# A fused attention and two-MLP kernel: early stage by batch, operand tile 384 bytes further on

## The chip, the cores and the metric

One core of one Trainium2 chip runs the whole program. The metric is device time in microseconds of one execution; a profiled execution gives the trace, in which the span runs from the first to the last instruction. Engines: PE (TensorE, matmuls), DVE (VectorE), ACT (ScalarE), POOL (GpSimd), and SP, whose queue starts the transfers.

## The reference

Three layers follow each other. B = 4 batches, 8 heads, S = 576 rows, head size 64, 32 memory slots; then NT = 2304 tokens of width 512.

```python
a = softmax(phi, axis=2)                        # b h s m, over m
k_m = einsum('bhsm,bhsd->bhmd', a, k); v_m = einsum('bhsm,bhsd->bhmd', a, v)
attn = softmax(q @ k_m.T / 8, axis=-1)          # over the 32 slots
x = (attn @ v_m)                                # -> 2304 x 512 tokens
x = relu(x @ w_in)**2 @ w_out                   # d_ff = 2048, weights are float64
p = probs / sum(probs)
out = sum_e p[:, e] * (relu(x @ w1[e]) @ w2[e]) # 4 experts, d_ff = 1024 each
```

## The kernel before, in words

Products of full precision are made of fp32r matmuls: an operand x is kept as a high part and a remainder (`put`, `split`), and a product is three matmuls (high·high, high·rest, rest·high).

**Early stage (slab 0).** The eight groups g are (batch, half of the heads). `front(g)` (F in the program string) loads phi, K/V and q, makes the memory (lines 121 to 163) and the scores: two halves z of 288 columns, each into a PSUM bank with the tag "score", of which there is one, and from there by a DVE transpose into `st` (line 173). Step B is the rest of the group: maximum, subtract (line 177), exponential, sum, reciprocal, multiply (line 185), transpose to `at` (line 189), the high part (ACT, line 191) and the remainder (DVE, line 192) into `mem`. Step A is `fold(0, b)`, which multiplies the first weights into the values of batch b. Step U j is the first MLP's slab 0 on half a batch (j = 0 and 1 are batch 0, and so on): `first_l1` (line 320) reads the attention tile of both groups of the batch, and the second layer `first_l2` (line 342) of a step is issued behind the first layer of the next one. Step W converts one chunk of 128x512 float64 weights to fp32 (`from_f64`, seven DVE instructions, lines 206 to 218) and, for the second layer, splits it (lines 231, 232). `PROGRAM` is the order in which these steps are written; the layer that builds the program then interleaves them on each engine, and each engine runs its list strictly in order. `FIRST_LOADS` is the order of the first transfers on the one queue of SP (p = phi, q, r = raw float64 weights, k = K/V).

**Slabs 1 to 4** of the first MLP follow, with `fold(s, b)` for each slab (line 296; its results leave PSUM through ACT line 302 and DVE line 303).

**Second stage.** The second MLP runs in two passes of 16 slabs. `second_pair` multiplies seven combinations of input blocks (moving operand, 512 columns, in the slots of `mem`) with seven combinations of weights (stationary, line 470); `second_l2` (line 431) has the second weights as the moving operand (512 columns, tiles `w` of other pools) and the activations `g` as the stationary one; `second_rest` (line 516) takes the last 256 columns, also out of `mem`. GpSimd makes the weight combinations (lines 266 to 269).

`mem`, one tile of 73,728 bytes per partition, holds the attention and the folded weights in the first MLP, and the slots of the second. The pool `const` hands out its tiles one behind the other: `ident` (512 bytes), `mem`, `acc`, and then the two small tiles of the probabilities.

Of the kernel before, what the change touches and what calls it, by code (L numbers as in the profile page):

```python
# [12 lines left out]
F32 = mybir.dt.float32  # L13
F32R = mybir.dt.float32r
AF = mybir.ActivationFunctionType
ALU = mybir.AluOpType
AX = mybir.AxisListType
I32 = mybir.dt.int32
U32 = mybir.dt.uint32

B, H, S, D, M = 4, 8, 576, 64, 32
NT, DM, DFF, E, F2 = 2304, 512, 2048, 4, 1024
KT = DM // 128
NG = 8
WC = 512
# [13 lines left out]
def tile_kernel(  # L39
# [10 lines left out]
    nc = tc.nc  # L50
    const = ctx.enter_context(tc.tile_pool(name="const", bufs=1))
    wcp = ctx.enter_context(tc.tile_pool(name="wcp", bufs=8))
# [7 lines left out]
    def bank(tag):  # L60
        return ps.tile([128, 512], F32, tag=tag, name=tag, bufs=BANKS[tag])

    ident = const.tile([128, 128], F32, name="ident")
    make_identity(nc, ident)

# [3 lines left out]
    atts = [a[:, 0] for a in area]  # L71
# [1 line left out]
    slot = [mem[:, i * 4 * NB:(i + 1) * 4 * NB] for i in range(9)]  # L73
    acc = const.tile([128, NT * KT], F32, name="acc")
    yacc = acc.rearrange("p (k n) -> p k n", k=KT)
    p_sb = const.tile([128, NT // 128, E], F32, name="p_sb")
    p_sum = const.tile([128, NT // 128], F32, name="p_sum")


    FIRST_LOADS = "p0 q0 r0 k0 p1 r1 k1 q1 r2 r3"  # L80

    PROGRAM = (
        "F0 W W F1 B0 A0 B1 F2 U0 W W F3 U1 B2 A1 B3 F4 U2 F5 U3 W B4 A2 B5 F6 U4 W F7 U5 "
        "B6 A3 B7 W U6 W U7"
    )


    CH = [(r * 128, min(128, S - r * 128)) for r in range((S + 127) // 128)]  # L90
# [5 lines left out]

    def load_kv(att, g):
        kvt = []
        for c, (s0, n) in enumerate(CH):
            if g == 0 and c < KT:  # L100
                t = yacc[:, c, S:S + 8 * D].rearrange("p (z h d) -> p z h d", z=2, h=4)
            else:
                t = att.tile([128, 2, 4, D], F32, tag="kv", name=f"kv{g}_{c}", bufs=5)
            nc.sync.dma_start(out=t[:n], in_=kv[g, s0:s0 + n].rearrange("s (z h d) -> s z h d", z=2, h=4))
            kvt.append(t)
        return kvt
# [10 lines left out]
    def attention(att, g):  # L117
        b, hg = divmod(g, 2)
        ph, kvt, qt = phs[g], kvs[g], qs[g]
        nmax = att.tile([128, 1], F32, tag="nmax", name="nmax")  # L120
        nc.vector.tensor_reduce(out=nmax, in_=ph, axis=AX.X, op=ALU.max, negate=True)
        esum = att.tile([128, 1], F32, tag="esum", name="esum")
        nc.scalar.activation(ph, ph, AF.Exp, bias=nmax, scale=1.0, accum_out=esum)
        rs = att.tile([128, 1], F32, tag="rs", name="rs")
        nc.vector.tensor_scalar_add(rs, esum, 1e-9)
        nc.vector.reciprocal(rs, rs)
        en = att.tile([128, len(CH), 128], F32, tag="en", name="en", bufs=1)
        pa = bank("turn")
        pb = bank("memory")
        for c, (s0, n) in enumerate(CH):  # L130
            dst = pa[:n, c * 128:(c + 1) * 128] if c < 4 else pb[:n, :128]
            nc.tensor.transpose(dst, ph[:, s0:s0 + n], ident)
        nc.scalar.copy(en[:, 0:4].rearrange("p c m -> p (c m)"), pa)
        nlast = CH[-1][1]
        nc.scalar.copy(en[:nlast, 4], pb[:nlast, :128])
        kvp = pb[:, 128:256]
        for c, (s0, n) in enumerate(CH):
            for h in range(4):
                nc.tensor.matmul(  # L139
                    kvp[h * M:(h + 1) * M, :2 * D],  # L140
                    en[:n, c, h * M:(h + 1) * M],
                    kvt[c][:n, :, h, :],
                    start=(c == 0),
                    stop=(c == len(CH) - 1),
                )


        kvd = att.tile([128, 2, 2, D], F32, tag="kvd", name="kvd", bufs=1)
        nc.scalar.activation(
            kvd,  # L150
            kvp.rearrange("p (v d) -> p v d", v=2).unsqueeze(2).to_broadcast([128, 2, 2, D]),
            AF.Copy, scale=rs,
        )
        kt = pb[:, 256:512]
        for v in range(2):
            nc.tensor.transpose(kt[:, v * 128:(v + 1) * 128], kvd[:, v].rearrange("p z d -> p (z d)"), ident)
        bt = bdk[g % 2]
        ktv = kt.rearrange("p (v z e m) -> p v z e m", v=2, z=2, e=2)
        for e in range(2):
            rows = slice(e * D, (e + 1) * D)  # L160
            nc.scalar.copy(bt[rows, :, e * M:(e + 1) * M], ktv[rows, 0, :, e, :])
        rows = slice(hg * D, (hg + 1) * D)
        nc.scalar.copy(vt[rows, b], kt[rows, 128:])
        st = att.tile([128, S // 32, 32], F32, tag="st", name="st", bufs=2)
        stf = st.rearrange("p j m -> p (j m)")
        for z in range(2):
            sc = bank("score")
            for pr in range(2):
                nc.tensor.matmul(
                    sc[pr * 64:(pr + 1) * 64, :HS], bt[:, pr, :], qt[pr][:, z * HS:(z + 1) * HS],  # L170
                    start=True, stop=True,
                )
            nc.vector.transpose(out=stf[:, z * HS:(z + 1) * HS], in_=sc[:, :HS])
        yield
        mx = att.tile([128, S // 32], F32, tag="mx", name="mx")
        nc.vector.reduce_max(out=mx, in_=st, axis=AX.X)
        nc.vector.tensor_tensor(
            out=st, in0=st, in1=mx.unsqueeze(2).to_broadcast([128, S // 32, 32]), op=ALU.subtract
        )
        nc.scalar.activation(st, st, AF.Exp, scale=1.0 / math.sqrt(D))  # L180
        sm = att.tile([128, S // 32], F32, tag="sm", name="sm")
        nc.vector.reduce_sum(out=sm, in_=st, axis=AX.X)
        nc.vector.tensor_scalar_add(sm, sm, 1e-9)
        nc.vector.reciprocal(sm, sm)
        nc.vector.tensor_tensor(
            out=st, in0=st, in1=sm.unsqueeze(2).to_broadcast([128, S // 32, 32]), op=ALU.mult
        )
        at = att.tile([128, S], F32, tag="at", name="at", bufs=1)
        nc.vector.transpose(out=at, in_=stf)
        hi = atts[b][:, hg]  # L190
        nc.scalar.copy(hi, at)  # L191
        nc.vector.tensor_tensor(out=atts[b][:, 2 + hg], in0=at, in1=hi.bitcast(F32), op=ALU.subtract)

# [4 lines left out]
    def from_f64(r, w):  # L200
        lo, hi = r[:, :, 0], r[:, :, 1]
        m = cv.tile([128, WC], F32, tag="cm", name="cm")
        a = cv.tile([128, WC], U32, tag="ca", name="ca")
        if w is None:
            w = a.bitcast(F32)
        nc.vector.tensor_scalar(m.bitcast(U32), hi, 0x7FFFFFFF, None, op0=ALU.bitwise_and)
        nc.vector.tensor_scalar(m, m, F_MIN, F_MAX, op0=ALU.max, op1=ALU.min)
        nc.vector.tensor_scalar(
            a, m.bitcast(U32), 3, 0x3FFFFFFF, op0=ALU.logical_shift_left, op1=ALU.bitwise_and
        )  # L210
        nc.vector.scalar_tensor_tensor(
            out=a, in0=hi, scalar=0xC0000000, in1=a, op0=ALU.bitwise_and, op1=ALU.bitwise_or
        )
        nc.vector.tensor_scalar(m.bitcast(U32), a, 0xFF800000, None, op0=ALU.bitwise_and)
        nc.vector.scalar_tensor_tensor(
            out=m, in0=lo, scalar=2.0 ** -52, in1=m, op0=ALU.mult, op1=ALU.mult
        )
        nc.vector.tensor_tensor(out=w, in0=a.bitcast(F32), in1=m, op=ALU.add)
        return w
# [312 lines left out]
    phs, kvs, qs, raws = {}, {}, {}, {}  # L532
# [7 lines left out]
    with tc.tile_pool(name="bdp", bufs=1) as bdp, tc.tile_pool(name="cv", bufs=1) as cv, \  # L540
# [6 lines left out]
        with tc.tile_pool(name="att", bufs=2) as att, tc.tile_pool(name="hp1", bufs=2) as hp, \  # L547
                tc.tile_pool(name="tmp1", bufs=1) as tmp:
            at = {}

            def front(g):
                if g not in phs:
                    phs[g] = load_phi(att, g)
                if g not in kvs:
                    kvs[g] = load_kv(att, g)
                if g not in qs:
                    qs[g] = load_q(g)
                at[g] = attention(att, g)
                next(at[g])

            for t in FIRST_LOADS.split():
                i = int(t[1])
                if t[0] == "p":
                    phs[i] = load_phi(att, i)
                elif t[0] == "k":
                    kvs[i] = load_kv(att, i)
                elif t[0] == "q":
                    qs[i] = load_q(i)
                else:
                    raws[i] = load64(i)  # L570
            for t in PROGRAM.split():
                i = int(t[1]) if len(t) > 1 else 0
# [17 lines left out]
            out=p_sb, in0=p_sb, in1=p_sum.unsqueeze(2).to_broadcast([128, NT // 128, E]), op=ALU.mult  # L590
# [98 lines left out]
```

## Time and profile before

| | before |
|---|---|
| median of 3 runs | 1167.53 us (1166.3 to 1167.62) |
| profiled execution | 1166.94 us; span 1164.9 us; granted clock 0.994 |
| PE busy / DVE / ACT / POOL | 98% / 72% / 42% / 10% |
| PE busy, 20 to 60 us | 30.94 of 40.00 us |
| PE busy, 440 to 700 us | 260.00 of 260.00 us |

A profile is read from the stretches: PE's busy time is modelled for pipelined matmuls, so that a busy PE need not run at its full rate. The rate is seen from the starts of successive matmuls. Where PE isn't busy, the row of the instruction behind the gap says what ended the wait.

### The profile page before, as it was taken

The page shows a single profiled execution, that of the slowest core. Times are in us where ns is not written, and L with a number is a line of the kernel's source. Part 1 is how long each engine was busy: PE and PEld are TensorE (multiplying, and loading weights), DVE is VectorE, ACT ScalarE, POOL GpSimd, SP SyncE. Part 2 cuts the span into 40 slices and gives each one's busy share as a digit, 9 for nine tenths or more (in the row PEclk, how much of TensorE's full clock was granted, in tenths as well). Part 3 has the DMA queues.
Part 4 walks back from the last instruction along what each step waited for, and adds up shares of the span by engine and source line. Part 5 has one row for each costly group of instructions (what it writes and reads, how often), then busy time and mean ns, then how long its engine had stood idle before and what let it go on. Part 6 is the DMA issues. An engine that isn't in the chain of part 4 may idle for free.

```text
span 1164.9 us, 16690 instructions
## 1 busy us (share of the span) xinstructions
PE 1139.3 (98%) x6520; PEld 957.9 (82%) x6520; DVE 839.0 (72%) x1442; ACT 494.9 (42%) x1051; POOL 121.3 (10%) x136
## 2 busy tenths in 40 slices
PE   5899999999999999999999999999999999999998
PEld 2676898999999988888888888888888888888886
DVE  5988999887457667777777778856666666666654
ACT  2666555544466563343433434543333333332321
POOL 0000000001010022121121211211111111121000
PEclk9799999999999999999999999999999999999999
DMA  9751222211000111111111111311111111111002
GB/s 313 237 184 37 73 74 91 74 55 55 1 19 1 54 46 64 37 55 55 55 55 37 55 55 53 110 37 37 37 37 54 37 55 37 37 37 37 19 1 91
DMA packets 25599, 72.68 MB, mean 62 GB/s; under 512 B 2992, under 2 KB 3504, under 8 KB 25520
## 3 DMA queue, kind: packets, MB, share of 16 engines
q1 hardware_dynamic: 25520, 71.61, 18.5%
q8 instruction: 51, 0.84, 0.3%
q14 instruction: 28, 0.23, 0.1%
HBM read 66.88 MB, written 4.72 MB: 61 GB/s over the span
## 4 chain that ended last, share of the span: by engine, by line
PE 91%; DVE 6%; ACT 1%; issue 1%; DMA 1%; SPq 0%; ACTq 0%
PE moe L470 23%; PE fold L431 17%; PE memory L431 8%; PE moe L342 8%; PE turn L431 8%; PE moe L320 4%; PE moe L516 4%; PE score L470 4%; PE turn L342 2%; PE score L342 2%; PE memory L342 2%; PE fold L296 2%; PE memory L320 1%; PE score L320 1%; PE memory L139 1%; DVE acc L350 1%
## 5 line engine op out<-in xcount | busy, mean ns | idle before, releaser
L431 PE MATMUL fold<-w,g 128*128 128x512 f32 x864 | 221.4, 391 | 0.0
L470 PE MATMUL moe<-mem,ws 128*128 128x512 f32 x768 | 201.4, 397 | 0.8 <-DVE c L478 0.8
L431 PEld LDWEIGHTS fold<-w,g 128*128 128x128 f32 x864 | 160.2, 188 | 33.2
L470 PEld LDWEIGHTS moe<-mem,ws 128*128 128x128 f32 x768 | 142.7, 188 | 37.9 <-DVE c L478 5.4
L342 PE MATMUL moe<-gh,wo 128*128 128x288 f32 x576 | 130.8, 298 | 1.2 <-ACT acc L348 0.7
L442 DVE SCALAR_TENSOR_TENSOR acc<-fold,p_sb,acc 128x512 f32<-128x512 f32 x135 | 100.8, 747 | 40.4 <-PE fold L431 40.2
L266 POOL TENSOR_TENSOR s<-ra 128x256 f32<-128x256 f32 x32 | 27.2, 850 | 951.5 <-DVE ws L232 391.3
L483 ACT COPY cc<-moe 128x512 f32<-128x512 f32 x96 | 56.1, 584 | 149.6 <-PE moe L470 149.4
L431 PE MATMUL turn<-w,g 128*128 128x512 f32 x432 | 110.1, 390 | 0.0
L431 PE MATMUL memory<-w,g 128*128 128x512 f32 x432 | 109.9, 390 | 0.0
L452 DVE SCALAR_TENSOR_TENSOR g<-c,g 128x512 fp32r<-128x512 f32 x128 | 97.4, 779 | 16.2 <-ACT g L451 11.8
L451 ACT ACTIVATE g<-c 128x512 fp32r<-128x512 f32 x128 | 80.3, 633 | 67.5 <-DVE c L478 66.8
L478 DVE TENSOR_TENSOR c<-moe,cc 128x512 f32<-128x512 f32 x96 | 66.0, 688 | 57.1 <-ACT cc L483 37.0
L342 PEld LDWEIGHTS moe<-gh,wo 128*128 128x128 f32 x576 | 97.4, 189 | 6.5 <-ACT acc L348 2.5
L431 PEld LDWEIGHTS turn<-w,g 128*128 128x128 f32 x432 | 81.1, 188 | 17.4
L431 PEld LDWEIGHTS memory<-w,g 128*128 128x128 f32 x432 | 81.1, 188 | 17.4
L470 PE MATMUL moe<-mem,w 128*128 128x512 f32 x384 | 95.3, 395 | 0.0
L470 PEld LDWEIGHTS moe<-mem,w 128*128 128x128 f32 x384 | 71.9, 188 | 17.0 <-ACT cc L483 0.2
L342 PE MATMUL moe<-gl,wo 128*128 128x288 f32 x288 | 85.6, 297 | 0.0
L320 PE MATMUL moe<-mem 128*128 128x288 f32 x432 | 75.3, 307 | 7.4 <-ACT mem L191 7.4
L231 ACT CAST w<-rb 128x512 fp32r<-128x512 f32 x64 | 39.9, 623 | 97.5 <-PE memory L431 65.8
L320 PEld LDWEIGHTS moe<-mem 128*128 128x128 f32 x432 | 62.3, 192 | 20.8 <-issue 9.8
(119 smaller groups left out, 1830.3 us busy)
## 6 DMA issues: line engine op xcount, KB each, us to landing
ra<-in_wts SPq DMA_DIRECT2D x32, 512.0 KB, 3.5
rb<-in_wts SPq DMA_DIRECT2D x32, 512.0 KB, 3.5
raw<-in_wts SPq DMA_DIRECT2D x28, 512.0 KB, 3.4
kv<-in_kv SPq DMA_DIRECT2D x28, 256.0 KB, 4.8
acc<-in_qT SPq DMA_DIRECT2D x16, 288.0 KB, 5.2
out<-acc SPq DMA_DIRECT2D x18, 256.0 KB, 2.0
ph<-in_phiT SPq DMA_DIRECT2D x8, 288.0 KB, 4.6
acc<-in_wts SPq DMA_DIRECT2D x4, 512.0 KB, 6.1
```

The costliest lines, as they stand in the source:

```text
L231: nc.scalar.copy(t[:, 0], w)
L266: nc.gpsimd.tensor_tensor(out=t[:, 0], in0=a21, in1=a22, op=ALU.add)
L320: nc.tensor.matmul(ph[:, :HS], folded[b][:, lw + hg, fc], atts[b][:, rx + hg, cs], start=(i == 0), stop=(i == 5))
L342: nc.tensor.matmul(po[:, :HS], w[:, lw], rg[:, f], start=(i == 0), stop=(i == 3 * nf - 1))
L431: nc.tensor.matmul(po, g[f][:, lg, at:at + 128], w[:, rw], start=(i == 0), stop=(i == 3 * NF2 - 1))
L442: nc.vector.scalar_tensor_tensor(out=oa, in0=src, scalar=pe, in1=oa, op0=ALU.mult, op1=ALU.add)
L451: nc.scalar.activation(g[:, 0, :n], c, AF.Relu)
L452: nc.vector.scalar_tensor_tensor(out=g[:, 1, :n], in0=c, scalar=0.0, in1=g[:, 0, :n].bitcast(F32), op0=ALU.max, op1=ALU.subtract)
L470: nc.tensor.matmul(po, wb[lw][k], xb[:, rx, k], start=(first and i == 0), stop=(i == 5), skip_group_check=not first,)
L478: nc.vector.tensor_tensor(out=c, in0=p, in1=q, op=ALU.add)
L483: nc.scalar.copy(c, p)
L516: nc.tensor.matmul(ph[:, :NR], w[f][:, lw, k * 128:(k + 1) * 128], x[:, rx, k], start=(i == 0), stop=(i == 3 * KT - 1),)
```

## The change

- `PROGRAM` is rewritten: two fronts, then both groups' B, then two steps U, batch by batch; four conversions W stand ahead of A0.
- `FIRST_LOADS`: both phi first, q of group 0 behind its K/V. The K/V of group 1 goes to three free weight buffers in place of the `kv` buffers.
- Scores: the second half of a group goes to a bank with the tag "fold", no longer to the one with the tag "score".
- For groups 4 to 7 the subtract, the multiply and the remainder run on GpSimd; for group 3 the multiply does.
- `from_f64`: the first DVE instruction of a chunk (clear the sign bit) becomes an ACT activation Abs.
- The tiles of the probabilities are taken ahead of `mem`. In the built program `mem` then starts at byte 17,408 of a partition (17 x 1024) in place of 17,024 (16 x 1024 + 640), and `acc` at 91,136 in place of 90,752. The tiles of the other pools keep their places: the weight buffers start at 128,000 (125 x 1024), the second stage's `g` at 201,728 (197 x 1024).

```diff
+    p_sb = const.tile([128, NT // 128, E], F32, name="p_sb")
+    p_sum = const.tile([128, NT // 128], F32, name="p_sum")
...
-    p_sb = const.tile([128, NT // 128, E], F32, name="p_sb")
-    p_sum = const.tile([128, NT // 128], F32, name="p_sum")
...
-    FIRST_LOADS = "p0 q0 r0 k0 p1 r1 k1 q1 r2 r3"
+    FIRST_LOADS = "p0 p1 r0 k0 r1 q0 k1 q1 r2 r3"
...
-        "F0 W W F1 B0 A0 B1 F2 U0 W W F3 U1 B2 A1 B3 F4 U2 F5 U3 W B4 A2 B5 F6 U4 W F7 U5 "
-        "B6 A3 B7 W U6 W U7"
+        "F0 W W F1 W W A0 B0 B1 F2 F3 U0 U1 A1 B2 B3 F4 W B4 F5 A2 W B5 U2 U3 W F6 F7 U4 B6 W "
+        "B7 A3 U5 U6 U7"
...
+        if g == 1:
+            spare = [
+                wcp.tile([128, 2, WC], F32, tag="wc", name=f"kvs{i}") for i in range((len(CH) + 1) // 2)
+            ]
...
+            elif g == 1:
+                t = spare[c // 2][:, c % 2].rearrange("p (z h d) -> p z h d", z=2, h=4)
...
-            sc = bank("score")
+            sc = bank("score" if z == 0 else "fold")
...
-        nc.vector.tensor_tensor(
+        (nc.gpsimd if g >= 4 else nc.vector).tensor_tensor(
             out=st, in0=st, in1=mx.unsqueeze(2).to_broadcast([128, S // 32, 32]), op=ALU.subtract
...
-        nc.vector.tensor_tensor(
+        (nc.gpsimd if g >= 3 else nc.vector).tensor_tensor(
             out=st, in0=st, in1=sm.unsqueeze(2).to_broadcast([128, S // 32, 32]), op=ALU.mult
...
-        nc.vector.tensor_tensor(out=atts[b][:, 2 + hg], in0=at, in1=hi.bitcast(F32), op=ALU.subtract)
+        (nc.gpsimd if g >= 4 else nc.vector).tensor_tensor(out=atts[b][:, 2 + hg], in0=at, in1=hi.bitcast(F32), op=ALU.subtract)
...
-        nc.vector.tensor_scalar(m.bitcast(U32), hi, 0x7FFFFFFF, None, op0=ALU.bitwise_and)
+        nc.scalar.activation(m, hi.bitcast(F32), AF.Abs)
```

DVE's list before, from group 0's `at` to that of group 1 (the first and the last row; `st_244` is group 1, `ph2` the phi of group 2, `cm` and `ca` a weight chunk under conversion):

```order
L189 STREAM_TRANSPOSE at_262<-st_171 128x576
L121 TENSOR_REDUCE nmax_307<-ph2_293 128x1
L182 TENSOR_REDUCE sm_284<-st_244 128x18
L192 TENSOR_TENSOR mem_72<-at_262,mem_72 128x576
L183 TENSOR_SCALAR sm_284<-sm_284 128x18
L125 TENSOR_SCALAR rs_311<-esum_309 128x1
L207 TENSOR_SCALAR cm_388<-cm_388 128x512
L184 RECIPROCAL sm_284<-sm_284 128x18
L126 RECIPROCAL rs_311<-rs_311 128x1
L208 TENSOR_SCALAR ca_389<-cm_388 128x512
L185 TENSOR_TENSOR st_244<-st_244,sm_284 128x576
L211 SCALAR_TENSOR_TENSOR ca_389<-acc_73,ca_389 128x512
L189 STREAM_TRANSPOSE at_289<-st_244 128x576
```

The same place of DVE's list in the changed kernel, where group 1 is `st_242`, and its `at` comes 19 rows behind that of group 0 (a row of "..." where seven of weights and group 1 are left out):

```order
L195 STREAM_TRANSPOSE at_298<-st_169 128x576
L217 SCALAR_TENSOR_TENSOR ca_252<-acc_75,ca_252 128x512
L182 TENSOR_REDUCE mx_302<-st_242 128x18
L220 TENSOR_SCALAR cm_251<-ca_252 128x512
L198 TENSOR_TENSOR mem_74<-at_298,mem_74 128x576
L221 SCALAR_TENSOR_TENSOR cm_251<-acc_75,cm_251 128x512
L183 TENSOR_TENSOR st_242<-st_242,mx_302 128x576
L224 TENSOR_TENSOR ca_252<-ca_252,cm_251 128x512
L127 TENSOR_REDUCE nmax_329<-ph2_315 128x1
L188 TENSOR_REDUCE sm_306<-st_242 128x18
...
L191 TENSOR_TENSOR st_242<-st_242,sm_306 128x576
L195 STREAM_TRANSPOSE at_311<-st_242 128x576
```

Before, 11 rows lie between the two `at`; now it is 18, among them the conversion of two weight chunks, group 1's maximum and subtract, and the phi of group 2.

PE's list before, at the folds of slab 1 (`fold_1388` and up, weights `wf_835` and `wf_1014`) in the last steps of slab 0; `moe_1207` and `moe_1220` are the first layer of U6, `moe_1233` the second layer of U5, `score_1459` a first layer of slab 1:

```order
L296 MATMUL fold_1388<-wf_835,vt_87 32x256 x2
L296 MATMUL fold_1388<-wf_1014,vt_87 32x256 x2
L320 MATMUL score_1459<-mem_72 128x288
L296 MATMUL fold_1389<-wf_835,vt_87 32x256 x2
L320 MATMUL moe_1207<-mem_72 128x288
L320 MATMUL moe_1220<-mem_72 128x288
L342 MATMUL moe_1233<-gh_1091,wo0_2_397 128x288
L342 MATMUL moe_1233<-gl_1092,wo0_2_397 128x288
```

The same folds in the changed kernel (`fold_1386`, `fold_1387`), between the second layer of U4 (`moe_1193`, `moe_1201`); rows that repeat are left out:

```order
L348 MATMUL moe_1193<-gh_1043,wo0_3_272 128x288
L302 MATMUL fold_1386<-wf_646,vt_87 32x256
L302 MATMUL fold_1387<-wf_646,vt_87 32x256
...
L302 MATMUL fold_1386<-wf_752,vt_87 32x256
L302 MATMUL fold_1387<-wf_752,vt_87 32x256
...
L348 MATMUL moe_1201<-gh_1043,wo0_2_260 128x288
L348 MATMUL moe_1201<-gl_1044,wo0_2_260 128x288
```

The folds of slab 1 for the first batch stood among pieces of three products, a few at a time; now all eight folds of the batch (two passes each on the chip) stand together, the two banks in turn.

GpSimd's list in the changed kernel, from its first softmax step on (`st_440` is group 3, `st_635` group 4, `st_727` group 5):

```order
L191 TENSOR_TENSOR st_440<-st_440,sm_568 128x576
L183 TENSOR_TENSOR st_635<-st_635,mx_656 128x576
L191 TENSOR_TENSOR st_635<-st_635,sm_660 128x576
L198 TENSOR_TENSOR mem_74<-at_665,mem_74 128x576
L183 TENSOR_TENSOR st_727<-st_727,mx_762 128x576
L191 TENSOR_TENSOR st_727<-st_727,sm_766 128x576
L198 TENSOR_TENSOR mem_74<-at_771,mem_74 128x576
```

Before, GpSimd had nothing in this stage. Now the six steps of batch 2 (the last six rows) follow each other, and the remainder of group 4 is ahead of the subtract of group 5.

## Rows read from the trace of the kernel before

**Rows 1.** Busy us (x count) by stretch: PE, PEld, DVE, ACT, POOL; PEclk; DMA share, GB/s.

```profile
20.00:60.00 40.00, 30.94 (x284) 20.66 (x278) 35.99 (x81) 23.16 (x61) 0.00 (x0) 0.83 0.78 259
93.70:110.00 16.30, 14.35 (x111) 9.13 (x111) 13.55 (x29) 9.06 (x22) 0.00 (x0) 1.00 0.10 34
120.00:200.00 80.00, 79.03 (x623) 71.37 (x622) 78.14 (x176) 44.01 (x116) 0.00 (x0) 1.00 0.24 79
440.00:700.00 260.00, 260.00 (x1133) 212.32 (x1132) 196.80 (x276) 96.53 (x162) 52.68 (x51) 1.00 0.16 51
```

**Rows 2.** TensorE in order of time, second stage: start us, length us, count.

```profile
708.69 1.56 PE L470 MATMUL moe<-mem,ws 128*128 128x512 f32 x6
710.09 1.54 PE L431 MATMUL fold<-w,g 128*128 128x512 f32 x6
711.46 1.52 PE L431 MATMUL turn<-w,g 128*128 128x512 f32 x6
712.82 0.39 PE L431 MATMUL fold<-w,g 128*128 128x512 f32 x1
```

**Rows 3.** Line L470, then line L516, from 400 us on: PE, PEld; PEclk; DMA.

```profile
400.00:1165.00 765.00, 328.02 (x1344) 250.65 (x1344) 1.00 0.14 47
...
400.00:1165.00 765.00, 53.52 (x384) 51.27 (x384) 1.00 0.14 47
```

**Rows 4.** 288-column matmuls by line and form, 250 to 400 us.

```profile
L342 PE MATMUL moe<-gh,wo 128*128 128x288 f32 x248 | 54.5, 295 | 0.0
...
L320 PE MATMUL moe<-mem 128*128 128x288 f32 x174 | 28.1, 297 | 0.0
```

**Rows 5.** TensorE in order of time, early; brackets: idle before, and releaser.

```profile
29.81 1.09 PE L320 MATMUL moe<-mem 128*128 128x288 f32 x3 [4.54 <-ACT mem L191]
...
34.86 1.06 PE L320 MATMUL moe<-mem 128*128 128x288 f32 x6
...
52.13 0.85 PE L320 MATMUL moe<-mem 128*128 128x288 f32 x2 [2.89 <-ACT mem L191]
```

**Rows 6.** VectorE in order of time, early.

```profile
18.80 0.48 DVE L173 STREAM_TRANSPOSE st<-score 128x288 f32<-128x288 f32 x1 [1.44 <-PE score L169]
...
28.29 0.77 DVE L189 STREAM_TRANSPOSE at<-st 128x576 f32<-128x576 f32 x1
...
33.20 0.77 DVE L189 STREAM_TRANSPOSE at<-st 128x576 f32<-128x576 f32 x1
...
46.48 0.69 DVE L232 TENSOR_TENSOR wo<-ca,wo 128x512 fp32r<-128x512 f32 x1
```

**Rows 7.** VectorE groups by form, first 200 us: count, busy us, mean ns.

```profile
L206 DVE TENSOR_SCALAR cm<-raw 128x512 uint32<-128x512 uint32 x19 | 8.0, 420 | 0.2
...
L185 DVE TENSOR_TENSOR st<-st,sm 128x576 f32<-128x576 f32 x8 | 6.0, 746 | 0.0
```

**Rows 8.** TensorE groups, 93.7 to 110 us, the folds among them.

```profile
L296 PE MATMUL fold<-wf,vt 64*32 64x256 f32 x54 | 5.7, 388 | 1.0 <-DVE mem L303 1.0
L342 PE MATMUL moe<-gh,wo 128*128 128x288 f32 x18 | 4.8, 312 | 0.5 <-ACT acc L348 0.5
L320 PE MATMUL moe<-mem 128*128 128x288 f32 x24 | 4.1, 304 | 0.0
L342 PE MATMUL moe<-gl,wo 128*128 128x288 f32 x9 | 2.7, 295 | 0.0
...
117.22 0.66 PE L296 MATMUL fold<-wf,vt 64*32 64x256 f32 x14
```

**Rows 9.** VectorE and GpSimd groups by form, from 400 us on.

```profile
L232 DVE TENSOR_TENSOR w<-ra,w 128x512 fp32r<-128x512 f32 x62 | 56.6, 924 | 18.6 <-ACT w L231 18.4
...
L232 DVE TENSOR_TENSOR w<-rb,w 128x512 fp32r<-128x512 f32 x60 | 41.8, 697 | 18.6 <-ACT w L231 18.6
...
L268 POOL TENSOR_TENSOR s<-ra 128x256 f32<-128x256 f32 x30 | 34.5, 1149 | 0.0
...
L266 POOL TENSOR_TENSOR s<-ra 128x256 f32<-128x256 f32 x30 | 25.3, 842 | 622.0 <-DVE ws L232 391.3 <-DMA ra<-in_wts 230.7
```

## Prediction

> **What bounds the kernel now.** I read the busy time by stretch first. From 440 to 700 us PE is busy for all of 260.00 us, DVE for 196.80 [rows 1]: there the time is the number of matmuls times their pitch. The early stage is another matter. From 20 to 60 us PE has 30.94 of 40 us, DVE 35.99, and the granted clock is 0.83, so for about a third of these 40 us PE ran at 1.2 GHz [rows 1]. From 120 to 200 us DVE has 78.14 of 80 us, but PE has 79.03 [rows 1]. So I look for two things: what sets the pitch in the second stage, and where PE waits before 200 us.
>
> *Pitch.* The starts of groups of six tell it: L470 goes from 708.69 to 710.09, 1.40 us or 233 ns each; L431 from 710.09 to 711.46 and on to 712.82, 2.73 us for twelve or 228 ns [rows 2]. Both have 512 columns and a full array. What differs is where the moving operand lies: L470 streams it from `mem`, which starts 640 bytes past a multiple of 1024, L431 from weight buffers that start on a multiple of 1024. L470 has 1344 matmuls, L516 (256 columns, also from `mem`) 384 [rows 3].
>
> *Early waits.* U0 starts at 29.81 behind the high part of group 0's attention (4.54 us idle), its half for group 1 at 34.86, U2 at 52.13 behind the same line (2.89 us idle) [rows 5]. These are DVE's softmax chains: `at` of group 0 starts at 28.29, that of group 1 at 33.20 [rows 6]. Later, "busy" hides the loss. From 93.7 to 110 us PE shows 14.35 of 16.30 us [rows 1], but it ran at least 51 products of 288 columns and 54 folds [rows 8]. At a steady 133 ns (1.40/6 scaled by 288/512 gives 131) and at most 47 ns for a fold (0.66 us for 14 [rows 8]) that is 6.8 + 2.5 = 9.3 us. Some 7 us of this stretch are lost, to folds that wait for their two banks and to the remainders of groups 6 and 7.
>
> **The change part by part.**
>
> *The tile's place.* If the pitch of L470 falls to that of L431, it gives 233 − 228 = 5 to 6 ns on 1344, so 6.7 to 8.1 us, all on the path. L516 would give another 2 us if it lost the same on 384; nothing shows that it does. Against it: the 288-column products start to end take 295 ns from `gh` and 297 from `mem` [rows 4], although they start at many offsets; but 1152 bytes cross one multiple of 1024 from any start here, 2048 bytes cross one from an aligned start and two from 640, so this is what the place would predict as well. Bounds 0 and 10; I take 7.5, nearest to what row 2 shows for the aligned stream.
> The Trainium skill (Advanced Engine Details and Errata, SBUF Cachelines) speaks against this: it knows lines of 16 bytes alone. Both old and new start are multiples of 64, and by that rule nothing changes; this is rival B, and no row here shows another reason for L470's pitch.
>
> *Start, to the first U.* The second half of group 0's scores is transposed at 18.80, after 1.44 us of waiting for PE [rows 6]; with a second bank it follows the first half directly. I put U0's first product 1.5 to 2 us earlier, near 28 us. q behind K/V costs nothing: the set of transfers ahead of group 1's K/V is the same.
>
> *From U0 to U2.* DVE's list now has 18 rows between the two `at` where there were 11. By the rows, these 18 are eight of about 0.67 us (576 columns: 746 ns [rows 7] less the overlap), five of 0.6, four of 0.34 to 0.42 and small ones: about 9 us, against 33.20 − 28.29 = 4.9. Less the 2 us gained ahead, U0's half for group 1 comes 2 us later than 34.86. What is done in the meantime isn't lost: the two second-layer weights, of which the last is split at 46.48 before [rows 6], are ready some 7 us earlier and out of the way of groups 2 and 3. So I see U2 again at 52, as before. Sum to there: 0, between −3 and +3; a stretch at 1.2 GHz more or less is in that.
>
> *Groups 3 to 7 and Abs.* DVE loses one step of 0.75 us for group 3 and three for each of groups 4 to 7, 13 in all or 9.7 us [rows 7], and 0.42 us [rows 7] for each of the 32 chunks, four of them by U0 and some five in slab 0 after U2, 2 us. On GpSimd a 128x256 step takes 842 to 1149 ns in the mean [rows 9]; a step of 576 columns, scaled, 1.9 to 2.6 us, less if part of it is fixed. It isn't free for DVE either: `w<-ra` beside GpSimd's work takes 924 ns, `w<-rb` without it 697 [rows 9], so 0.23 us in the mean, 3 us for 13 steps. Net about 9 us of DVE are freed between 57 and 117 us.
> The Trainium skill (SBUF — State Buffer, Who interferes with whom) says that a DVE instruction with two SBUF inputs and a GpSimd one that reads SBUF exclude each other, the second fully blocked until the first ends. By that rule alone each step could hold DVE for its whole 1.9 to 2.6 us, 25 to 34 us in all; the row's 0.23 us of delay on a mean of 0.92 shows far less.
>
> *What PE gets of it.* Abs and the GpSimd steps are off PE; they count only where PE waits. The folds of slab 1 stand together now, behind the second layer of U4, with no first layer between that shares their wait. I expect about 5 of the 7 us between 93.7 and 110 back, and 2 us in the neighbouring stretches and to 200 us, where the conversions held DVE at 98%. Given back: U4 waits for GpSimd's remainder of group 5. Two groups' six steps run in one queue; I count about 2 us of idle PE at U4 and 1 us at U6. Net −5 to −6, between 0 and −11. The work that hides GpSimd is the second layer of the step before (24 products, 3.2 us); without it each GpSimd step costs its own length.
>
> **Sum** against the profiled execution, 1166.94 us (2.0 around the span): −7.5 for the place, 0 to U2, −5.7 after it: 1153.7. The median of the runs shown is 0.6 above the profiled one: **1154**.
>
> **Rivals.**
> - *B, the place does nothing* (24%). L470 stays at 233 ns, only the early stage gains: 1167.5 − 5.7 = 1162. For it: the 288-column rows don't tell places apart. Against: two streams of equal shape with a steady 5 ns between them.
> - *C, GpSimd's queue becomes the bound at U4 and U6* (8%, slower). At the upper row, 2.6 us a step, the six steps of a batch take 15.5 us where DVE's took 4.5, 11 more; some 3 are hidden. PE, in order, then stands 8 us at U4 and again at U6: 16 us, the gain of the folds gone: 1167.5 − 7.5 + 16 = 1176. The point from which it decides: 12 steps × (t − 0.75) less 6 hidden passes 7.5 us at t = 1.9 us. It is the lower row's scaled value, but these rows hold DVE's interference and a fixed part, and the stalls overlap with K/V work, so I keep it small.
> - *D, the change only moves waits* (8%): nothing from the place, and what the folds gain is lost at U0 and U4: 1167.
>
> **How the numbers follow.** My forecast (A) has 60%, its own range 1147 to 1161 (place 5 to 10, early stage 0 to 11). The range for 8 in 10 takes in most of B, whose early gain of 3 gives 1164.5, and leaves out C, D and the ends of A: 1146.5 to 1164.5. About 0.2% (2.3 us) is what a measurement of this kernel tells from no change. Faster by more than that: A, nearly all of B, 85%; within: D less a little, 7%; slower: C, 8%.
>
> **What would show it.** In the profile after: groups of six of L470 1.36 to 1.37 us apart (B if 1.40). L516 unchanged or 2 us less in all. U0's first product near 28 us, U2's near 52. The sixteen passes of a fold batch together in about 0.6 us. GpSimd's 576-column steps at 1.4 to 1.9 us; above that C begins, seen as idle PE before the second half of U4 that GpSimd's line 198 ends. The prediction is wrong if U2 is more than 3 us late, if PE's clock drops for a further stretch before 60 us, or if L470's pitch has another cause than its tile's place.

## The result

The changed kernel takes 1151.71 us in the median (1151.28 to 1153.41, four runs), the kernel before 1167.16 (1166.30 to 1167.62, four runs): ratio 0.9869, 95% interval 0.9858 to 0.9881, 15.5 us less where 13.5 were forecast. The profiled execution took 1151.41 us (span 1149.3).

The first product of the second stage that reads `mem` cuts the span in two. These are the rows of that line (count, ns min/median/max, first and last start), first the kernel before, then the changed one, where line 470 is now 476 and 431 is 437:

```profile
L470 PE MATMUL moe<-mem,w x384: 387/394/414, 403.6 to 1139.8; 128*128 128x512 f32 x192
L476 PE MATMUL moe<-mem,w x384: 387/389/410, 396.5 to 1124.5; 128*128 128x512 f32 x192
```

The early stage is 403.6 − 396.5 = 7.1 us shorter, the rest of the span 761.3 − 752.8 = 8.5 us. Both halves of the forecast came (5.7 and 7.5), and each is looked at by itself.

**Second stage.** TensorE in order of time, changed kernel:

```profile
700.00 1.52 PE L437 MATMUL turn<-w,g 128*128 128x512 f32 x6
701.36 1.52 PE L437 MATMUL fold<-w,g 128*128 128x512 f32 x6
702.72 1.52 PE L437 MATMUL memory<-w,g 128*128 128x512 f32 x6
704.08 1.52 PE L476 MATMUL moe<-mem,ws 128*128 128x512 f32 x6
705.44 0.84 PE L437 MATMUL fold<-w,g 128*128 128x512 f32 x3
```

Six products from `mem` now take 705.44 − 704.08 = 1.36 us, 227 ns each, like six from the weight buffers; in [rows 2] they took 1.40. On 1344 products, 233 − 227 is 8 us.

**Early stage.** The windows of [rows 1] again, with 60 to 120 us added (same columns):

```profile
20.00:60.00 40.00, 32.23 (x318) 21.28 (x315) 35.52 (x77) 25.98 (x68) 2.60 (x2) 0.76 0.79 259
60.00:120.00 60.00, 55.77 (x499) 44.98 (x499) 55.54 (x116) 44.85 (x121) 14.83 (x12) 1.00 0.37 121
93.70:110.00 16.30, 15.26 (x117) 13.51 (x116) 13.92 (x25) 11.76 (x31) 1.75 (x2) 1.00 0.25 75
120.00:200.00 80.00, 79.72 (x634) 72.83 (x633) 75.88 (x164) 50.82 (x127) 0.00 (x0) 1.00 0.24 80
440.00:700.00 260.00, 260.00 (x1149) 215.28 (x1148) 200.40 (x283) 101.98 (x171) 53.68 (x52) 1.00 0.15 51
```

From 20 to 60 us PE gets through 318 products where it had 284, at a lower granted clock (0.76 against 0.83); but most of the 34 more are small ones of the fronts, which the changed kernel does earlier (320 of all 440 are started by 60 us, 272 before). In 440 to 700 us it is busy throughout as before, but does 1149 products, not 1133.

TensorE in order of time, to be held against [rows 5]; `fold<-wf` at 90.83 is the fold of slab 1 for the first batch:

```profile
26.15 1.09 PE L326 MATMUL moe<-mem 128*128 128x288 f32 x3 [2.84 <-ACT mem L197]
...
35.97 1.09 PE L326 MATMUL moe<-mem 128*128 128x288 f32 x3
...
50.71 0.54 PE L326 MATMUL moe<-mem 128*128 128x288 f32 x2 [1.24 <-ACT mem L197]
...
77.05 0.54 PE L326 MATMUL moe<-mem 128*128 128x288 f32 x2 [1.13 <-POOL mem L198]
...
90.83 0.99 PE L302 MATMUL fold<-wf,vt 64*32 64x256 f32 x16 [0.27 <-DVE mem L309]
...
97.52 0.80 PE L326 MATMUL moe<-mem 128*128 128x288 f32 x4 [0.43 <-POOL mem L198]
```

U0 starts 3.7 us earlier than before, its half for group 1 1.1 us later, U2 1.4 us earlier; the sixteen passes of the first batch's fold of slab 1 stand together. VectorE in order of time:

```profile
15.38 0.48 DVE L179 STREAM_TRANSPOSE st<-score 128x288 f32<-128x288 f32 x1
15.78 0.44 DVE L179 STREAM_TRANSPOSE st<-fold 128x288 f32<-128x288 f32 x1
...
24.62 0.77 DVE L195 STREAM_TRANSPOSE at<-st 128x576 f32<-128x576 f32 x1
...
33.88 0.77 DVE L195 STREAM_TRANSPOSE at<-st 128x576 f32<-128x576 f32 x1
```

The second score transpose follows the first at 15.78; in [rows 6] it came at 18.80. The two `at` are 9.3 us apart (4.9 before). GpSimd's groups by form, first 200 us (count, busy us, mean ns, idle before):

```profile
L198 POOL TENSOR_TENSOR mem<-at,mem 128x576 fp32r<-128x576 f32 x4 | 6.2, 1553 | 6.1 <-ACT mem L197 6.1
L191 POOL TENSOR_TENSOR st<-st,sm 128x576 f32<-128x576 f32 x5 | 6.1, 1213 | 62.5 <-DVE sm L190 59.2 <-ACT g L333 3.3
L183 POOL TENSOR_TENSOR st<-st,mx 128x576 f32<-128x576 f32 x4 | 5.2, 1308 | 9.8 <-DVE mx L182 9.8
```

So the new steps cost GpSimd 1.2 to 1.6 us in the mean where VectorE needed 0.75 [rows 7].

### The profile page after: what moved, and what is told of

The parts are those of the page before. It is cut to its first block, busy times and chain, and to the rows that moved or that the text cites. A ratio compares the mean times of both kernels' runs of the same rounds, so it can differ in the third digit from the quotient of the medians.

```text
span 1149.3 us, 16715 instructions
## 1 busy us (share of the span) xinstructions
PE 1121.4 (98%) x6520; PEld 956.3 (83%) x6520; DVE 826.7 (72%) x1397; ACT 510.8 (44%) x1083; POOL 138.3 (12%) x149
## 4 chain that ended last, share of the span: by engine, by line
PE 89%; DVE 6%; DMA 2%; ACT 1%; issue 1%; POOL 1%; SPq 0%; POOLq 0%; ACTq 0%
PE moe L476 23%; PE fold L437 17%; PE memory L437 9%; PE turn L437 8%; PE moe L348 8%; PE moe L326 4%; PE moe L522 4%; PE score L476 4%; PE turn L348 3%; PE score L348 2%; PE memory L348 2%; PE memory L326 1%; PE fold L302 1%; PE score L326 1%; DMA acc<-in_qT 1%; DMA acc<-in_wts 1%
## 5 line engine op out<-in xcount | busy, mean ns | idle before, releaser
L476 PE MATMUL moe<-mem,ws 128*128 128x512 f32 x768 | 197.3, 392 | 1.2 <-DVE c L484 1.2
L476 PE MATMUL moe<-mem,w 128*128 128x512 f32 x384 | 93.0, 389 | 0.0
L335 DVE TENSOR_TENSOR gl<-g,gh 128x288 fp32r<-128x288 f32 x128 | 63.1, 494 | 28.6 <-ACT gh L334 28.2
```

The costliest lines, as they stand in the source:

```text
L335: nc.vector.tensor_tensor(out=gl[:, f], in0=g, in1=gh[:, f].bitcast(F32), op=ALU.subtract)
L476: nc.tensor.matmul(po, wb[lw][k], xb[:, rx, k], start=(first and i == 0), stop=(i == 5), skip_group_check=not first,)
```

## The experiments

Three theories were open after the result: that the tile's place gives the second stage's gain and nothing else; that the early gain comes from each of Abs, the second bank, GpSimd and the order by itself, as the prediction summed them; or that these work only together. All kernels are measured beside the kernel before (medians 1166.8 to 1167.2). "Rest" is the profiled span less the start of the second stage; both columns come from the one profiled execution, which need not be the median one.

| kernel | median us (lowest, highest) | ratio [95%] | second stage starts | rest |
|---|---|---|---|---|
| changed | 1151.71 (1151.28, 1153.41) | 0.9869 [0.9858, 0.9881] | 396.5 | 752.8 |
| place alone | 1158.70 (1158.18, 1160.14) | 0.9930 [0.9916, 0.9945] | 403.5 | 752.7 |
| place undone | 1160.04 (1159.04, 1161.35) | 0.9938 [0.9925, 0.9951] | 397.4 | 761.5 |
| start at 128 | 1160.77 (1159.81, 1161.70) | 0.9943 [0.9929, 0.9957] | 396.5 | 761.4 |
| start at 256 | 1151.51 (1150.85, 1153.26) | 0.9866 [0.9851, 0.9881] | 396.3 | 752.9 |
| softmax on VectorE | 1155.04 (1153.07, 1156.15) | 0.9896 [0.9883, 0.9909] | 398.4 | 752.7 |
| sign on VectorE | 1161.45 (1159.22, 1162.57) | 0.9951 [0.9939, 0.9963] | 404.7 | 752.7 |
| one score bank | 1161.49 (1157.89, 1163.17) | 0.9947 [0.9932, 0.9961] | 407.5 | 752.7 |
| old program | 1154.12 (1153.54, 1154.80) | 0.9889 [0.9875, 0.9904] | 399.8 | 752.7 |
| program alone | 1164.64 (1162.18, 1170.97) | 0.9977 [0.9963, 0.9990] | 409.9 | 752.7 |
| Abs alone | 1153.86 (1152.58, 1155.53) | 0.9887 [0.9873, 0.9901] | 400.3 | 753.2 |
| bank alone | 1155.15 (1154.84, 1155.85) | 0.9898 [0.9885, 0.9911] | 400.1 | 752.9 |
| first remainders on GpSimd | 1152.55 (1150.91, 1155.46) | 0.9878 [0.9862, 0.9894] | 400.7 | 752.9 |

### The tile's place

Place alone: the kernel before, with the two small tiles taken ahead of `mem`.

```diff
     make_identity(nc, ident)
+    p_sb = const.tile([128, NT // 128, E], F32, name="p_sb")
+    p_sum = const.tile([128, NT // 128], F32, name="p_sum")
```

> The kernel before with the probability tiles ahead of the operand tile and nothing else changed. If the place of the tile sets the pitch, the 512-column products that stream from it start 227 to 228 ns apart in place of 233, and the time falls by 1344 x 5.7 ns, 7.6 us (6.5 to 8.5), to about 1159.5 us. Rival (the pitch comes from the early program or from what runs beside the products): 233 ns and no change, 1167 us.

Measured: 8.1 us less than before; the early stage is as it was (403.5), the whole gain is in the rest.

Place undone: the changed kernel, with those two tiles behind `acc` again.

```diff
     make_identity(nc, ident)
-    p_sb = const.tile([128, NT // 128, E], F32, name="p_sb")
-    p_sum = const.tile([128, NT // 128], F32, name="p_sum")
...
     yacc = acc.rearrange("p (k n) -> p k n", k=KT)
+    p_sb = const.tile([128, NT // 128, E], F32, name="p_sb")
+    p_sum = const.tile([128, NT // 128], F32, name="p_sum")
```

> The changed kernel with the probability tiles behind the operand tile again, which puts it back at byte 17,024. Place theory: 233 ns, 7.6 us slower than the changed kernel, about 1159.3 us; early stage as in the changed kernel, so 7.5 to 8 us faster than before. Rival: 227 ns, no change, 1151.7 us. If the two parts were not independent, the two gains would not add up to 15.5 us.

Measured: 8.3 us more than the changed kernel. In the profiled executions the rest is 8.7 us longer and the early stage 0.9 us.

Start at 128, and start at 256: the changed kernel, with a pad of so many bytes ahead of `mem` and what is missing to 1024 behind `acc`, so that only `mem` and `acc` move against the multiples of 1024. The edit for 128; for 256 the pads have 64 and 192 columns.

```diff
+    pad_a = const.tile([128, 32], F32, name="pad_a")
...
     yacc = acc.rearrange("p (k n) -> p k n", k=KT)
+    pad_b = const.tile([128, 224], F32, name="pad_b")
```

> The changed kernel with the operand tile 128 bytes further on (128 past a multiple of 1024; the other pools stay on multiples of 1024). Before, it lay 640 past one, which is also 128 past a multiple of 256 and of 512. If any start off a multiple of 1024, 512 or 256 costs, 233 ns again and about 1159.3 us. If only the distance 640 costs, 227 ns and 1151.7 us.

> The changed kernel with the operand tile 256 bytes further on. If multiples of 1024 or of 512 are wanted (a product that crosses one boundary more costs 6 ns), 233 ns and 1159.3 us. If a multiple of 256 is enough, 227 ns and 1151.7 us.

TensorE groups by form from 400 us on, start at 128 and then start at 256 (line 470 is 478 here):

```profile
L439 PE MATMUL fold<-w,g 128*128 128x512 f32 x864 | 221.4, 391 | 0.0
L478 PE MATMUL moe<-mem,ws 128*128 128x512 f32 x766 | 200.9, 397 | 1.1 <-DVE c L486 1.1
```

```profile
L439 PE MATMUL fold<-w,g 128*128 128x512 f32 x864 | 220.6, 390 | 0.0
L478 PE MATMUL moe<-mem,ws 128*128 128x512 f32 x765 | 196.6, 392 | 1.2 <-DVE c L486 1.2
```

128 bytes past the boundary bring all of the old cost back (397 ns start to end, rest 761.4), 256 bytes past it none (392 ns, rest 752.9). That `acc` moves too changes nothing where it is written: VectorE's `acc<-fold` takes 747 ns in the kernel before and 746 in the changed one.

### The parts of the early stage, one taken out at a time

Softmax on VectorE: the three steps return from GpSimd to VectorE for all groups.

```diff
-        (nc.gpsimd if g >= 4 else nc.vector).tensor_tensor(
+        nc.vector.tensor_tensor(
...
-        (nc.gpsimd if g >= 3 else nc.vector).tensor_tensor(
+        nc.vector.tensor_tensor(
...
-        (nc.gpsimd if g >= 4 else nc.vector).tensor_tensor(out=atts[b][:, 2 + hg], in0=at, in1=hi.bitcast(F32), op=ALU.subtract)
+        nc.vector.tensor_tensor(out=atts[b][:, 2 + hg], in0=at, in1=hi.bitcast(F32), op=ALU.subtract)
```

> The changed kernel with the softmax steps of groups 3 to 7 back on VectorE. If GpSimd helps by freeing VectorE, 2 us slower than the changed kernel (0 to 4), 1153.5 us. Rival (GpSimd's longer steps sit in the chain that PE waits for, at the second half of U4 and U6): 1 to 2 us faster, 1150 us, and the two waits behind GpSimd's remainder (1.6 us in the changed kernel's trace) become shorter.

Measured: 3.3 us more than the changed kernel. GpSimd's part helps; the size is near the expectation. The ranges just touch (1153.07 and 1153.41), and in the profiled executions the second stage starts only 1.9 us later.

Sign on VectorE, and one score bank:

```diff
-        nc.scalar.activation(m, hi.bitcast(F32), AF.Abs)
+        nc.vector.tensor_scalar(m.bitcast(U32), hi, 0x7FFFFFFF, None, op0=ALU.bitwise_and)
```

> The changed kernel with the sign cleared on VectorE again (32 instructions of 0.42 us). If VectorE's time counts in the early stage, 1 to 2 us slower, 1153 us, above all between 20 and 60 us. Rival (Abs at the head of ScalarE's list holds the exponentials up as much as it frees VectorE): no change, 1151.7 us.

```diff
-            sc = bank("score" if z == 0 else "fold")
+            sc = bank("score")
```

> The changed kernel with both halves of the scores in the one bank again. If the second bank takes a wait out of every group's chain, U0 starts 1.5 us later (26.15 us in the changed kernel) and the time is 1 to 2 us longer, 1153 us. Rival (the wait moves to the fold banks anyway): no change.

Measured: 9.7 and 9.8 us more than the changed kernel, several times what was expected of each. In the profiled executions, the shortest of five with the sign on VectorE and the second longest of six with one bank, the second stage starts 8.2 and 11.0 us later. Windows of TensorE alone, 60 to 120 us (us, busy us, count, PEclk, DMA, GB/s): the changed kernel, the sign on VectorE, one score bank, and the program alone, which comes further down:

```profile
60.00:120.00 60.00, 55.77 (x499) 1.00 0.37 121
60.00:120.00 60.00, 53.21 (x476) 0.97 0.40 127
60.00:120.00 60.00, 52.66 (x454) 0.97 0.36 119
60.00:120.00 60.00, 55.77 (x456) 0.91 0.32 106
```

Counts of all products mix large and small ones, so only those of 288 columns are compared here. By 60 us the changed kernel has started 68 of them, the other two 67 and 60 (and 30 and 28 fewer of the fronts' small ones); by 110 us 292, 258 and 225; by 390 us 2256, 2194 and 2174. The deficits of 62 and 82 at the end, at 133 ns each, are 8.2 and 10.9 us. Most of the loss lies behind 60 us, and not between 20 and 60 as was expected of the sign. With one bank the first part shows in the first product of U0:

```profile
29.80 1.09 PE L326 MATMUL moe<-mem 128*128 128x288 f32 x3 [2.95 <-ACT mem L197]
```

It starts at 29.80 in place of 26.15, 3.65 us later. (Executions differ here: with two banks and the new order U0 starts at 26.0 to 27.3 us, in one at 28.9.) The rest comes later: in the first 200 us VectorE waits 6.3 us for PE at the score transposes with one bank, 2.1 + 0.3 us (two groups) with two. The sign costs VectorE 23 instructions in the first 200 us, 10.7 us; the second stage comes 8.2 us later for it.

Old program: the changed kernel with the order of steps of before.

```diff
-        "F0 W W F1 W W A0 B0 B1 F2 F3 U0 U1 A1 B2 B3 F4 W B4 F5 A2 W B5 U2 U3 W F6 F7 U4 B6 W "
-        "B7 A3 U5 U6 U7"
+        "F0 W W F1 B0 A0 B1 F2 U0 W W F3 U1 B2 A1 B3 F4 U2 F5 U3 W B4 A2 B5 F6 U4 W F7 U5 "
+        "B6 A3 B7 W U6 W U7"
```

> The changed kernel with the old order of steps; everything else stays. If the order by batch is what gives the early stage its gain, 4 to 5 us slower, 1156 us, with folds of slab 1 among other products again between 90 and 115 us. Rival (the relief of VectorE and the banks give it): within 1.5 us of the changed kernel.

Measured: 2.4 us more than the changed kernel, about half of the expectation. `FIRST_LOADS` and the spare K/V buffers stay new here. From 93.7 to 110 us the clock was 0.90, where the changed kernel had 1.00.

### The parts alone

Each of these stands on the kernel of the place alone (1158.70 us). Program alone: the new `PROGRAM`, the new `FIRST_LOADS` and group 1's K/V in spare buffers; one score bank, sign and softmax on VectorE.

```diff
-    FIRST_LOADS = "p0 q0 r0 k0 p1 r1 k1 q1 r2 r3"
+    FIRST_LOADS = "p0 p1 r0 k0 r1 q0 k1 q1 r2 r3"
...
-        "F0 W W F1 B0 A0 B1 F2 U0 W W F3 U1 B2 A1 B3 F4 U2 F5 U3 W B4 A2 B5 F6 U4 W F7 U5 "
-        "B6 A3 B7 W U6 W U7"
+        "F0 W W F1 W W A0 B0 B1 F2 F3 U0 U1 A1 B2 B3 F4 W B4 F5 A2 W B5 U2 U3 W F6 F7 U4 B6 W "
+        "B7 A3 U5 U6 U7"
...
+            elif g == 1:
+                t = spare[c // 2][:, c % 2].rearrange("p (z h d) -> p z h d", z=2, h=4)
```

> The kernel before with the tile's new place, the new order of steps, the new first loads and the spare K/V buffers, but one bank for scores, the sign on VectorE and no softmax on GpSimd. Taken out of the changed kernel one at a time, the sign cost 9.7 us and the second bank 9.8 us, more together than the whole early gain of 8. If VectorE is what limits the early stage and the order by batch only pays once it is relieved, this kernel is slower than the tile's place alone (1158.7 us): 1163 to 1170 us. Rival (the order is good by itself, and each part only repairs a bad interleaving of its own): 1156 us.

Measured: 5.9 us slower than the place alone. VectorE's waits of the first 200 us, this kernel (us in total, times, longest), and the same line of the changed kernel:

```profile
DVE st L179 <- PE score L175: 9.4, 11, 2.1
```

```profile
DVE st L179 <- PE score L175: 2.1, 3, 1.1
```

The order by batch puts both groups' scores through one bank in a row; with the old order and one bank (place alone) these waits are 6.2 us. `FIRST_LOADS` and the spare buffers have no run of their own, so that the 5.9 us belong to the order together with them.

Abs alone, and bank alone, both in the old order:

```diff
-        nc.vector.tensor_scalar(m.bitcast(U32), hi, 0x7FFFFFFF, None, op0=ALU.bitwise_and)
+        nc.scalar.activation(m, hi.bitcast(F32), AF.Abs)
```

> The kernel before with the tile's new place and the sign on ScalarE, old order of steps. VectorE theory: 22 of the 32 instructions of 0.42 us lie in the first 200 us, 9.2 us of VectorE; where it is the limit a good part comes back: 3 to 6 us faster than the place alone, 1153 to 1156 us. Rival (the 9.7 us belong to the new order alone): within 1.5 us of 1158.7 us.

```diff
-            sc = bank("score")
+            sc = bank("score" if z == 0 else "fold")
```

> The kernel before with the tile's new place and the second half of the scores in a fold bank, old order of steps. VectorE waits 6.3 us in all for PE at the score transposes before; if the second bank takes most of that away also in the old order, 2 to 4 us faster than the place alone, 1155 to 1157 us. Rival (it only matters where two fronts stand one behind the other, as in the new order): 1158.7 us.

Measured: 4.8 us and 3.6 us less than the place alone. Both times came as expected, but VectorE's waits at the score transposes did not follow (Abs alone, then bank alone, where the fold bank adds 0.5 us):

```profile
DVE st L173 <- PE score L169: 7.7, 10, 3.1
DVE st L173 <- PE score L169: 3.7, 6, 1.3
```

With the place alone they are 6.2 us: the second bank takes 2 us of them away, not most, and Abs makes them longer and the kernel still faster.

First remainders on GpSimd: the changed kernel, and the subtract that splits slab 0's second-layer weights goes to GpSimd too.

```diff
-        nc.vector.tensor_tensor(out=t[:, 1], in0=w, in1=t[:, 0].bitcast(F32), op=ALU.subtract)
+        (eng or nc.vector).tensor_tensor(out=t[:, 1], in0=w, in1=t[:, 0].bitcast(F32), op=ALU.subtract)
...
-                    w_out[s].append(split(from_f64(r, None), f"wo{s}_{i}"))
+                    w_out[s].append(split(from_f64(r, None), f"wo{s}_{i}", eng=nc.gpsimd if s == 0 else None))
```

> The changed kernel with the remainders of slab 0's two second-layer weights (2 steps of 0.69 us, near 33 and 40 us) on GpSimd, which is idle there. If VectorE's time counts one for one in this stretch, 1 to 1.5 us faster than the changed kernel, 1150.4 us. Rival (the next chunk's conversion waits for GpSimd to have read the one scratch buffer, about 1.4 us each): no gain or 1 us slower.

Measured: no gain over the changed kernel (1152.55 against 1151.71, ranges overlap). Its profiled execution, the slowest of its four, starts the second stage 4.2 us later than the changed kernel, but 2.7 us of that are there at U0 (28.86 against 26.15), before the first moved step runs at 32.94; the moved steps didn't make them. Why there is no gain is open. PE had the full clock from 20 to 60 us here (1.00; 0.76 in the changed kernel), and the start at 256 (0.83) and at 128 (0.75) began the second stage at 396.3 and 396.5: the clock of that stretch doesn't decide between them.

**Where the early time is gained.** These rows count the products that TensorE had started by 110 us: first layer, second layer and folds, the kernel before and then the changed one (us, busy us, count, PEclk, DMA, GB/s).

```profile
0.00:110.00 110.00, 21.81 (x102) 0.94 0.61 199
0.00:110.00 110.00, 26.51 (x146) 0.94 0.61 199
0.00:110.00 110.00, 11.88 (x104) 0.94 0.61 199
```

```profile
0.00:110.00 110.00, 20.48 (x100) 0.91 0.64 210
0.00:110.00 110.00, 31.04 (x192) 0.91 0.64 210
0.00:110.00 110.00, 7.12 (x96) 0.91 0.64 210
```

At the prediction's 133 ns for 288 columns and 47 ns for a pass of a fold, the changed kernel is 44 x 0.133 − 8 x 0.047 = 5.5 us of work ahead. The same count at other times, and for the other kernels, is this estimate of the lead over the kernel before, in us. The fronts' small products are left out, so the first column is rough; all are done by 110 us. The last column, from the start of the second stage, shows that the count fits.

| kernel | by 80 us | by 93.7 | by 110 | by 200 | by 390 | second stage earlier by |
|---|---|---|---|---|---|---|
| changed | 0.1 | 1.5 | 5.5 | 7.3 | 7.0 | 7.1 |
| softmax on VectorE | 2.7 | 1.9 | 4.1 | 5.6 | 5.2 | 5.2 |
| sign on VectorE | −1.9 | −1.1 | −0.3 | −0.5 | −1.2 | −1.1 |
| one score bank | −3.5 | −4.5 | −4.2 | −2.2 | −3.9 | −3.9 |
| old program | 0.3 | 0.7 | 3.2 | 4.1 | 3.7 | 3.8 |
| program alone | 0.0 | −2.5 | −4.1 | −3.5 | −6.4 | −6.3 |
| Abs alone | 0.3 | 1.1 | 3.3 | 3.6 | 3.2 | 3.3 |
| bank alone | 2.8 | 2.5 | 4.1 | 3.7 | 3.3 | 3.5 |

The changed kernel gains most, 3.9 us, between 93.7 and 110 us.

## Why the forecast came out near

- **The tile's place, −7.5.** Right, shown both ways: 8.1 us put in alone, 8.3 taken out, and the rest of the span is 752.7 to 753.2 us in every kernel whose `mem` starts on a multiple of 256 bytes, 761.3 to 761.5 in the three where it starts 128 past one (640 is 2 x 256 + 128). The picture behind it was wrong: counting multiples of 1024 that a row crosses gives a cost to the start at 256, which has none. Line 516 (256 columns) gained nothing: 53.52 us [rows 3], now 53.36. The 864 products `fold<-w,g` went from 391 to 390 ns, 0.8 us in all, though their operands did not move; they follow the place (391 again at 128). That a little of a slow product falls on its neighbours would explain it, and isn't shown. Rival B fell. The Trainium skill (Advanced Engine Details and Errata, SBUF Cachelines) has lines of 16 bytes alone, by which the starts at 128 and 256 would be equal; they differ by 9.3 us, and the measurement decides. Why 128 past a multiple of 256 is slow, no run shows.
- **Start to U2, 0.** U0 came at 26.15, not 28: the bank's term was sized at 1.5 to 2 us, and without the bank U0 is 3.65 us later. Group 1's half at 35.97 (forecast 36.9) and 9.3 us between the two `at` (forecast 9) are as worked out. U2 is at 50.71, within the ±3, and by 80 us the lead is 0.1 us. The granted clock did drop for a longer stretch (0.76), which the prediction named as a way to be wrong; the stage gained anyway.
- **After U2, −5.7.** Right in size (7.1) and in place, partly by luck. Its own terms make 4, not 5.7: 5 and 2 given back, 2 and 1 of idle PE taken off. From 93.7 to 110 us the kernel before did 56 products of 288 columns (the prediction counted at least 51) and 54 passes of folds, the changed one 99 and 16: 13.9 us of work against 10.0, so 3.9 of the 5 us came. 1.5 us of lead were there at 93.7, 1.8 came between 110 and 200, and PE waited 1.6 us for GpSimd's remainder and not 3. The step that failed is the cause that was named, folds of slab 1 that stand together by the new order, with Abs and GpSimd for the 2 us around. In the old order the same stretch gives back 2.5 us with all the reliefs and 2.2 with Abs alone, where the folds still come in pieces of 2 to 12 passes. Abs is worth 4.8 us alone and 9.7 when taken out, the bank 3.6 and 9.8, the order 2.4 when taken out. What the standing together gives by itself, no run separates; the passes took 0.99 us at 90.83, not 0.6.
- **The terms cannot be summed.** The four early parts taken out singly (GpSimd 3.3, Abs 9.7, bank 9.8, order 2.4) make 25.2 us; all of them together, with the loads, are worth 1158.70 − 1151.71 = 7.0. The new order, with the loads, loses 5.9 us without the reliefs; with them, the order gains 2.4. So what each relief is worth depends on the order, and what the order is worth on the reliefs. Why is argued, not shown: one list in strict order, in which a late step holds up all behind it. VectorE's waits at the score transposes are only part of it: in the new order they are 9.4 us without any relief, 6.3 with all but the bank and 2.4 with all, but with the sign on VectorE they are 3.3, and that kernel is as slow as the one with one bank. The kernels also differ in the stretches at half clock (60 to 120 us: 1.00 changed, 0.97 in the two, 0.91 with the program alone), and no run holds the clock fixed.
- **GpSimd's queue.** Steps of 1.2 to 1.6 us against a forecast of 1.4 to 1.9; PE waits for line 198's remainder 1.13 us at U4 and 0.43 at U6, forecast 2 and 1. Rival C fell: without GpSimd the kernel is 3.3 us slower. What a step costs VectorE was sized too small. Two places in the changed kernel, GpSimd and VectorE:

```profile
72.53 1.16 POOL L191 TENSOR_TENSOR st<-st,sm 128x576 f32<-128x576 f32 x1 [3.27 <-ACT g L333]
72.58 1.42 DVE L335 TENSOR_TENSOR gl<-g,gh 128x288 fp32r<-128x288 f32 x1
...
96.04 1.43 POOL L198 TENSOR_TENSOR mem<-at,mem 128x576 fp32r<-128x576 f32 x1 [2.02 <-ACT mem L197]
96.19 1.57 DVE L220 TENSOR_SCALAR cm<-ca 128x512 uint32<-128x512 uint32 x1
```

These VectorE instructions take 0.45 and 0.42 us elsewhere; here both end 0.3 us after GpSimd's step. Eight are held like this, together 6.4 us where 3 were forecast, out of the 9.7 us that the thirteen steps take off VectorE; with the softmax on VectorE none is. The Trainium skill (SBUF — State Buffer, Who interferes with whom) has VectorE and GpSimd share one pair of ports as an exclusive lock, on which the later of two that contend is fully blocked. The trace agrees in each of the eight; the price stays below the 17.5 us that the thirteen steps last, and VectorE's maximum and sum over 576 columns and its transpose `at` ran beside GpSimd at their usual length (0.74 to 0.78 us).

- **Rival D** (waits only move) fell with the early stage's 7.1 us, though the program alone is nearly that case.

No version beat the changed kernel; the start at 256 equals it. The place and Abs alone, two edits of a line or two, give 13.3 of the 15.5 us.

## What to carry over

Look at where a streamed operand starts before looking at the order of work: the hint is a steady difference in pitch between two products of the same shape, and one kernel that moves the tile settles it. An order that puts two chains side by side paid here only with a second bank and a relieved VectorE; judge order and relief together, and test each alone and each taken out. When a forecast's sum is right, its terms can still be wrong: compare the work done by fixed times between kernels, and count products of one size only.

## What was not expected of the hardware

- A product of 128x512 f32 whose moving operand starts 128 bytes past a multiple of 256 is followed by the next after 233 ns, with starts at 0 and 256 past a multiple of 1024 after 227; products of 256 columns show no difference (282 ns start to end with the starts at 128 and 256). Starts other than 0, 128, 256 and 640 past a multiple of 1024 were not tried.
- GpSimd's subtract and multiply of 128x576 took 1.2 to 1.3 us, less than the 1.9 to 2.6 us that scaling the 128x256 steps of [rows 9] gave.
- GpSimd's steps held single VectorE instructions until they ended, 8 of them by 0.2 to 1.1 us each. Among these is one with a single SBUF operand, L220 (1.46 and 1.57 us in place of 0.42).
